# Seeding PSUM from ScalarE in both gates of an attention and gMLP kernel, with the scalings of weights and outputs on VectorE

## The chip, the core and the metric

The kernel runs on one core of a Trainium2 chip. The core has five engines that run side by side and meet through semaphores: TensorE (PE) multiplies matrices into PSUM, ScalarE (ACT) and VectorE (DVE) read and write PSUM and SBUF, GpSimd (POOL) works on SBUF, and SyncE (SP) issues most of the transfers. PSUM has eight banks of 128 x 512 float32. The metric is the device time of one execution in microseconds; lower is better.

## What is computed

Attention with a compressive memory over a layer-normalised input, added to the input; then a gated MLP over the layer-normalised sum, added again. The change lies in the second half, which is, cut to what matters:

```python
z = _gelu(jnp.einsum('bsd,df->bsf', x, w_in))        # x: 2048 x 1024, w_in: 1024 x 3584
z1 = z[..., :Fh].copy()                              # Fh = 1792
z2 = _layernorm(z[..., Fh:], axis=-1)
g = jnp.einsum('ts,bsf->btf', w_sp, z2) + b_sp[None, :, None]    # w_sp: 2048 x 2048
return jnp.einsum('bsf,fd->bsd', z1 * g, w_out)
```

So the "gate" is a product of the 2048 x 2048 matrix w_sp with z2, to which a bias per output token t is added, and which is then multiplied element by element with z1.

## The kernel before

**How the order comes about.** The program is written out once by Python code. Every call such as `act.activation(...)` or `pe.matmul(...)` goes through a recorder (lines 30 to 260), which appends it to the list of its engine and works out what it must wait for: results it reads, readers of what it overwrites, and for a PSUM bank any earlier access of another engine. Each engine then runs its own list strictly in the order recorded. A waiting instruction therefore holds up everything behind it on its engine. All instructions are issued at one line (L214), so the profile tells them apart by the names of their tiles.

**Stages.** Attention and the layer norms, then z2 and z1 (their input products, with gelu), then the first gate (`gate(0)`, output tokens 0 to 1023), four `out_unit`s that finish tokens 0 to 255, the second gate (`gate(1)`, tokens 1024 to 2047), and the output stage with the remaining tokens.

**The gate.** The product is done by a Strassen-Winograd scheme: seven block products where a plain 2 x 2 blocking needs eight. The weights are blocks of w_sp, called b11, b12, b21, b22, and their differences t1 to t4 (`sp_sum` in the first gate, `q_sum` in the second); the other operand is z2 in feature blocks of 128, of which `a_blk(i, j, g)` picks one, and sums of such blocks, SS[0] to SS[3] (`s_sum(1)` to `s_sum(4)`, DVE). Features are done in seven groups, g = 0 to 6. A product is eight matmuls of 128 x 128 by 128 x 512 into one bank. In the order of PE, a group has: t2 and t1, in groups 1 to 3 a p1 for a later group, t3, p2 of the next group, t4, b22. Banks rotate: three for p1/p2 (`g % 3`), two for t2, t3, t4 (`bb`), two for t1 and b22 (`bc`); bank 7 is left for sums of squares.

p1(g), the product with b11, is needed four times over. Before the change it goes this way:

- `copy1` (ACT) copies p1, scaled by `inv`, into `s1` (tile tmp_s) in SBUF; POOL adds the two halves of the bias row BROW to it and writes `s1b1` and `s1b2` (tile tmp_s1b).
- After t2, DVE's `stt` computes u2 = bank x inv + s1b2; after t3, u3 in the same way from the same bank (tile tmp_u). t3 adds on to the bank of t2, so it cannot start before u2 has read it, nor t4 before u3.
- The four outputs of a group are each a `stt` into VB, scaling a bank and adding u2, u3, s1b1 or BROW, followed by a multiplication with z1 (`out`), both on DVE. The first gate writes Z1T, the second Z1X.

`each(g, k)` with k = 0 to 3 are four places in each group where other work is put into the queues: in the first gate (`each0`) sums of squares of the gate's outputs (`z1_norm`) and of the output weights (`w_norm`), the loads of the second gate's blocks (`q_load`) and their scaling to float16 (`q_conv`); in the second gate (`each1`, from a table `jobs`) sums of squares of the finished outputs (`y0_norm`), their scale (`y0_scale`) and scaling (`y0_conv`), the scale of the output weights (`scale_w`), their loads (`ob_load`), scaling (`ob_scale`) and differences (`ob_sum`). The scales are powers of two that keep float16 in range.

**Between the gates**, `brow_sq` squares the new bias rows, `scale_y` derives YS and `INVY`, scales the rows by YS on ACT, and `q_conv` and `q_sum` prepare the remaining blocks.

**The output stage** uses the same scheme with seven matmuls a product: `o_p1(g)` is copied by ACT into a tile `ot`, POOL adds the residual to it three times (`o_adds`), `o_p2(g)` adds on to the same bank and `o_c11` evicts it. Before the change o_p2(0) follows o_p1(0) directly.

Of the kernel before, what the change touches and what calls it, by code (L numbers as in the profile page):

```python
# [262 lines left out]
def bass_sequential_preLN__memory_aug_infini_attn__mixer_gmlp__prompt_kernel(  # L263
# [24 lines left out]
    def tens(name, shape, dt, off):  # L288
        sz = int(np.prod(shape[1:])) * mybir.dt.size(dt)
        assert off % 32 == 0 and off + sz <= ARENA, (name, off, sz)  # L290
        t = nc.alloc_sbuf_tensor_at(name, list(shape), dt, offset=abase + off)
        R.space[t[:].tensor.name] = ("sbuf", off)
        return t

    class Bump:
# [4 lines left out]
        def __call__(self, name, shape, dt):  # L300
# [90 lines left out]
          for p, o in enumerate((162, 105))]  # L391
# [16 lines left out]
    SC = [b3("sc%d" % i, [128, 1], F32) for i in range(2)]  # L408
    INV = [b3("inv%d" % i, [128, 1], F32) for i in range(2)]
    TW, YS, INVY, SCW, INVO = [b3(k, [128, 1], F32) for k in ("tw", "ys", "invy", "scw", "invo")]  # L410
    SQY = tens("sqy", [128, 28], F32, 768)
    BSQ = tens("bsq", [128, 2], F32, 896)
    TMP = {k: tens("tmp_" + k, [128, L], F32, o * K)
           for k, o in zip(("s1", "s1b1", "s1b2", "u2", "u3"), (190, 192, 194, 196, 12))}
# [23 lines left out]
    def bank(b):  # L438
        return PS[:, b, :]
# [7 lines left out]
    free = []  # L447
# [768 lines left out]
        sp.dma_start(RAW1[k][:].rearrange("p j c n -> p j (c n)"), WSPT[Q4.index(k)])  # L1216

    def q_conv(k):
        if k == "b22":
            dve.tensor_single_scalar(BH1[k][:], RAW1[k][:], SC[0][:], ALU.mult)  # L1220
            return
        if k == "b21":
            dve.tensor_single_scalar(BH1[k][:, 0:2], RAW1[k][:, 0:2], SC[0][:], ALU.mult)
        for r in range(2 * (k == "b21"), 4):
            act.activation(BH1[k][:, r], RAW1[k][:, r], ACTF.Copy, scale=SC[0][:])
# [19 lines left out]
    def a_blk(i, j, g):  # L1245
        f = 896 * i + 128 * g
        return Z2H[:, 8 * j:8 * j + 8, f:f + 128]
# [8 lines left out]
        else:  # L1256
            dve.tensor_tensor(SS[:, 3], a_blk(0, 1, g), SS[:, 1], ALU.subtract)

    def gate(pr, seam=lambda: None, mid=lambda: None, each=lambda g, k: None):
# [4 lines left out]
        def prod(b, a, w, first):  # L1264
            for i in range(8):
                pe.matmul(bank(b), a[:, i, :], bh(w, i), start=(first and i == 0), stop=(i == 7),
                          skip_group_check=True)

        s1, s1b1, s1b2, u2, u3 = (TMP[k][:] for k in ("s1", "s1b1", "s1b2", "u2", "u3"))

        def stt(o, b, add):
            dve.scalar_tensor_tensor(o, bank(b), inv[:], add, ALU.mult, ALU.add)

        def out(v, g, i, t):
            dve.tensor_tensor(zo[:, g + 7 * i, t], v, Z1T[:, g + 7 * i, t], ALU.mult)

        def ss(k, g):
            if g < 7:
                s_sum(k, g)

        def p1(g):
            prod(g % 3, a_blk(0, 0, g), "b11", True)

        def copy1(g):
            act.activation(s1, bank(g % 3), ACTF.Copy, scale=inv[:])

        def p2(g):
            prod(g % 3, a_blk(0, 1, g), "b21", False)

        def c11(g):  # L1290
            stt(VB[:], g % 3, BROW[0][:])
            out(VB[:], g, 0, t1)

        p1(0)
        copy1(0)
        for o, k in ((s1b2, 1), (s1b1, 0)):
            (dve if pr else pool).tensor_tensor(o, s1, BROW[k][:], ALU.add)
        p1(1)
        p1(2)
        seam()  # L1300
        p2(0)
        c11(0)
        for g in range(7):
            bb, bc = 3 + g % 2, 5 + g % 2
            prod(bb, SS[:, 1], "t2", True)
            prod(bc, SS[:, 0], "t1", True)
            stt(u2, bb, s1b2)
# [9 lines left out]
            prod(bb, SS[:, 2], "t3", False)  # L1317
            if g < 5:
                copy1(g + 1)
                p2(g + 1)  # L1320
            elif g == 5:
                p1(6)
                copy1(6)
            else:
                p2(6)
            each(g, 1)
            stt(u3, bb, s1b2)
            stt(VB[:], bc, u3)
            out(VB[:], g, 1, t2)
            if not g:  # L1330
                ss(1, 1)
                ss(2, 1)
            if g < 6:
                pool.tensor_tensor(s1b2, s1, BROW[1][:], ALU.add)
            ss(3, g + 1)
            if g != 5:
                c11(min(g + 1, 6))
            prod(bb, a_blk(1, 1, g), "t4", False)
            each(g, 2)
            stt(VB[:], bb, s1b1)  # L1340
            out(VB[:], g, 1, t1)
            if g < 6:
                pool.tensor_tensor(s1b1, s1, BROW[0][:], ALU.add)
            prod(bc, SS[:, 3], "b22", False)
            stt(VB[:], bc, u2)
            out(VB[:], g, 0, t2)
# [82 lines left out]
    def on(g, k, f, *a):  # L1429
        todo1.setdefault((g, k), []).append((f, a))  # L1430
# [105 lines left out]

    def each0(g, k):
        z1_norm(g, k)
        for h, lo in ((1, 15), (0, 21)):
            for n in range(14):  # L1540
                if 4 * g + k == lo + n // 5:
                    w_norm(h, n)
            if 4 * g + k == lo + 2 and h:
# [6 lines left out]
        if (g, k) == (4, 0):  # L1550
            total(28, SQY, TOTY)
        if (g, k) == (6, 0):
            brow_in(1)
            q_load("b11")
            q_load("b12")
            q_conv("b11")
        if (g, k) == (6, 1):
            fin_load(units[1])
            w1_load(1)
            q_conv("b12")  # L1560
        if (g, k) == (6, 2):
# [14 lines left out]
    def scale_y():  # L1576
        power(YS)
        dve.tensor_tensor(INVY[:], INV[0][:], YS[:], ALU.mult)
        for k in range(2):
            act.activation(BROW[k][:], BROW[k][:], ACTF.Copy, scale=YS[:])  # L1580

    brow_sq()
    pool.tensor_tensor(TOT[:], TOTY[:], TW[:], ALU.mult)
    rot["banks"], rot["n"] = [0, 1, 2, 3], 0
    free.clear()
    q_sum("t1")
    for n, u in enumerate(units):
        out_unit(u, (lambda i: WO0[i // 7][:, i % 7, :]) if u[1] == 0 else
                 (lambda i: WO1[i // 7][:, i % 7, :]))
        if n == 0:  # L1590
            s_sum(1, 0)
            s_sum(2, 0)
        if n == 2:
            scale_y()
            q_conv("b21")
            q_sum("t3")
        if n == 1:
            q_conv("b22")
    q_sum("t2")
# [205 lines left out]
```

## Time and profile before

| | |
|---|---|
| median of three runs | 746.99 us (746.89 to 747.02) |
| the profiled execution | 747.36 us, of which its span (first to last instruction) 745.6 us |
| granted TensorE clock | 1.000 over the span |
| end of z1, start of the first gate | 483.9 us |
| first gate / units / second gate / output stage | 84.64 / 12.08 / 86.73 / 78.25 us |
| busy in the first gate: PE, DVE, ACT, POOL | 84.64, 68.03, 48.37, 19.43 us |
| busy in the second gate: PE, DVE, ACT, POOL | 85.36, 80.61, 44.32, 16.90 us |

The page lists groups of instructions as "out<-in xcount | busy us, mean ns | idle before, and what ended it". The timeline lists instructions as "start, duration, engine, line, what", in us from the span's start, with the idle time before an instruction and its releaser in brackets. Matmuls overlap, so a row's duration is longer than the distance to the next row; distances are read from start to start.

### The profile page before, as it was taken

To read this page: it belongs to the slowest core of one execution; us is meant where nothing else is said; L and a number is where in the kernel's file an instruction comes from. 1 tells how busy PE (TensorE), PEld (TensorE's weight loads), DVE (VectorE), ACT (ScalarE), POOL (GpSimd) and SP (SyncE) were. 2 spreads that over 40 slices of the span, in tenths; PEclk is the share of its full clock that TensorE was granted. 3 is DMA by queue.
4 is the path that set the end of the run, shared out by engine and by line. 5 is a ranking of instruction groups with operands and counts; after the bars stand their busy time and mean duration, and the time that the engine had idled before them with its cause. 6 is when DMAs were issued, how large, how long until landed. Compare 5 with 4: busy or idle time off the path is not lost.

```text
span 745.6 us, 13617 instructions
## 1 busy us (share of the span) xinstructions
PE 735.0 (99%) x5399; PEld 351.4 (47%) x5399; DVE 609.9 (82%) x1065; ACT 480.5 (64%) x656; POOL 307.7 (41%) x448
## 2 busy tenths in 40 slices
PE   8999999999999999999999999999999999999998
PEld 3454455545555445545554444444444444444444
DVE  5577889889988989879896777797885989987676
ACT  6777888888887888816886669846538687000000
POOL 2555456555654343110154899632220122224342
PEclk9999999999999999999999999999999999999999
DMA  9565668457635752644050037399638201031311
GB/s 295 178 171 121 140 143 179 130 148 165 171 99 162 250 177 58 178 120 128 29 141 1 1 57 127 68 193 189 200 117 307 71 22 36 1 114 63 106 57 57
DMA packets 148800, 92.65 MB, mean 124 GB/s; under 512 B 105984, under 2 KB 132864, under 8 KB 148224
## 3 DMA queue, kind: packets, MB, share of 16 engines
q1 hardware_dynamic: 147920, 91.00, 46.9%
q8 instruction: 42, 0.69, 0.4%
q10 hardware_dynamic: 816, 0.79, 0.3%
q14 instruction: 22, 0.18, 0.1%
HBM read 56.11 MB, written 12.58 MB: 92 GB/s over the span
## 4 chain that ended last, share of the span: by engine, by line
PE 84%; DVE 7%; ACT 3%; issue 3%; DMA 1%; POOL 1%; ACTq 0%; DVEq 0%; POOLq 0%
PE ps L214 84%; ACT ps L214 1%; DMA wv<-in_A_wv_dram 1%; DVE sqz L214 1%; DVE vb L214 1%; DVE stats L214 1%; ACT b12g L214 1%; DVE tmp_u L214 0%; ACT b11g L214 0%; DVE ss L214 0%; DVE z1x L214 0%; ACT e L214 0%; DVE hch L214 0%; POOL sz L214 0%; DVE tm L214 0%
## 5 line engine op out<-in xcount | busy, mean ns | idle before, releaser
L214 ACT ACTIVATE e<-ps 128x2048 bf16<-128x2048 f32 (+1 forms) x96 | 152.7, 1590 | 21.3 <-PE ps L214 20.6
L214 POOL TENSOR_SCALAR_AFFINE_SELECT e<-e 128x512 bf16<-128x512 bf16 x128 | 91.2, 726 | 123.1 <-ACT e L214 122.9
L214 POOL TENSOR_TENSOR tmp_s1b<-tmp_s,brow 128x512 f32<-128x512 f32 x26 | 33.9, 1305 | 104.5 <-DVE tmp_u L214 37.0
L214 PE MATMUL ps<-xnT,wk 128*128 128x512 bf16 x256 | 60.8, 380 | 0.6 <-ACT v L214 0.4
L214 PE MATMUL ps<-wv,xnT 128*128 128x512 bf16 x256 | 59.7, 380 | 1.3 <-DMA wv<-in_A_wv_dram 1.2
L214 PE MATMUL ps<-xnT,wq 128*128 128x512 bf16 x256 | 60.5, 379 | 0.0
L214 PE MATMUL ps<-wo,oT 128*128 128x512 bf16 x256 | 58.2, 380 | 0.8 <-DVE hch L214 0.8
L214 ACT ACTIVATE ot<-ps,invo 128x512 f32<-128x512 f32 x7 | 4.8, 687 | 70.6 <-PE ps L214 70.6
L214 POOL TENSOR_TENSOR ot<-ot,fin 128x512 f32<-128x512 f32 x21 | 27.9, 1352 | 47.1 <-ACT ot L214 47.1
L214 PEld LDWEIGHTS ps<-v,e 128*128 128x128 bf16 x1280 | 38.8, 96 | 14.0 <-issue 6.5
L214 PE MATMUL ps<-v,e 128*128 128x33 bf16 x1280 | 42.2, 178 | 0.0
L214 POOL TENSOR_TENSOR sz<-wzh 128x512 f16<-128x512 f16 x28 | 34.1, 1218 | 11.1 <-PE ps L214 11.1
L214 DVE BATCH_NORM_STATS2 zst<-z 128x6 f32<-128x448 bf16 x64 | 38.1, 609 | 0.0
L214 PEld LDWEIGHTS ps<-wo,oT 128*128 128x128 bf16 x256 | 24.0, 98 | 28.6 <-DVE hch L214 1.3
L214 PE MATMUL ps<-z2h,sy 128*128 128x512 f16 (+2 forms) x182 | 37.4, 363 | 0.0
L214 DVE TENSOR_TENSOR zt<-ps,zt 128x512 f32<-128x512 f32 x28 | 19.1, 686 | 22.1 <-PE ps L214 17.6
L214 PEld LDWEIGHTS ps<-xnT,wk 128*128 128x128 bf16 x256 | 22.6, 98 | 30.6 <-issue 4.5
L214 ACT ACTIVATE qk<-ps 128x512 bf16<-128x512 f32 x48 | 28.7, 598 | 12.9 <-PE ps L214 12.9
L214 PEld LDWEIGHTS ps<-wv,xnT 128*128 128x128 bf16 x256 | 23.2, 98 | 28.3 <-DMA wv<-in_A_wv_dram 1.9
L214 PE MATMUL ps<-qk 32*128 32x128 bf16 (+3 forms) x512 | 34.5, 302 | 0.7 <-DVE tm L214 0.5
L214 PEld LDWEIGHTS ps<-xnT,wq 128*128 128x128 bf16 x256 | 23.5, 98 | 22.9 <-issue 0.2
L214 ACT ACTIVATE z<-zp,inv 128x448 bf16<-128x448 f32 x28 | 18.6, 665 | 19.5 <-DVE zp L214 19.4
(284 smaller groups left out, 1712.7 us busy)
## 6 DMA issues: line engine op xcount, KB each, us to landing
nb<-in_B_w_in_dram SPq DMA_DIRECT2D x16, 448.0 KB, 4.1
nb<-in_B_w_sp_dram SPq DMA_DIRECT2D x14, 512.0 KB, 4.6
w_out<-in_B_w_out_dram SPq DMA_DIRECT2D x6, 896.0 KB, 5.9
xch<-in_A_x_dram SPq DMA_DIRECT2D x16, 256.0 KB, 4.6
xr<-in_A_x_dram SPq DMA_DIRECT2D x16, 256.0 KB, 3.9
out_dram<-hch SPq DMA_DIRECT2D x16, 256.0 KB, 2.4
w_spT<-stg SPq DMA_DIRECT2D x16, 256.0 KB, 4.2
out_dram<-fin SPq DMA_DIRECT2D x31, 128.0 KB, 1.7
```

The costliest lines, as they stand in the source:

```text
L214: ins = getattr(e, op.name)(*op.args, **op.kw)
```

## The change

In both gates the bias and the first product are no longer added outside PSUM. ACT writes a starting value into a bank (a seed), and every product accumulates on it (`start=False` throughout):

- `seed_a(g)`: BROW[0] times RINV into p1's bank, before p1(g). RINV is 1/INV[0], computed once in the z1 stage, so that the later scaling by inv gives the bias back; in the second gate INVY = INV[0] x YS scales it by YS as well, and the rows themselves are no longer scaled.
- `seed_b(g)`: p1's bank, seed included, copied to the bank of t2, t3 and t4.
- `seed_c(g)`: the difference of the two bias rows (`db`, computed once a gate by POOL) times RINV into the bank of t1 and b22.
- `copy_u(2, g)` and `copy_u(3, g)`: u2 and u3 become plain scaled copies on ACT. copy1, s1, s1b1 and s1b2 go.
- Of the four outputs of a group, the two of token half t1 become a single DVE instruction (bank x inv x z1); the two of half t2 stay a `stt` and a multiplication.
- The first two seeds of the first gate are issued in the z1 stage (`pre_seed`), into banks that are free by then. The gate's banks are taken from the list of free banks in their order (`perm`).
- In group 0 of the second gate the order of PE is t1, t2, p2(0), t3.
- All of `q_conv`, `ob_scale` and `y0_conv` move from ACT to DVE; `w_norm` is spread over more places (three for each instead of five) and begins one place earlier or later; the sum `total(28, SQY, TOTY)` moves from place (4, 0) to (4, 3); the scaling of b11 and b12 moves to (6, 2) and (6, 3); `q_sum("t3")` moves behind `s_sum(3, 0)`.
- In the output stage o_p2(0) and o_c11(0) move behind o_t4(0), as in the other groups.

```diff
+    RINV = tens("rinv", [128, 1], F32, 1024)
...
     def q_conv(k):
...
+        dve.tensor_single_scalar(BH1[k][:], RAW1[k][:], SC[0][:], ALU.mult)
...
+        def prod(b, a, w):
             for i in range(8):
+                pe.matmul(bank(b), a[:, i, :], bh(w, i), start=False, stop=(i == 7), skip_group_check=True)
...
+        def out(g, i, t, b, add=None):
+            o, z = zo[:, g + 7 * i, t], Z1T[:, g + 7 * i, t]
+            if add is None:
+                dve.scalar_tensor_tensor(o, bank(b), inv[:], z, ALU.mult, ALU.mult)
+            else:
+                dve.scalar_tensor_tensor(VB[:], bank(b), inv[:], add, ALU.mult, ALU.add)
+                dve.tensor_tensor(o, VB[:], z, ALU.mult)
...
+        def seed_a(g):
+            act.activation(bank(ba(g)), BROW[0][:], ACTF.Copy, scale=RINV[:])
+
+        def seed_b(g):
+            act.activation(bank(bb(g)), bank(ba(g)), ACTF.Copy)
+
+        def seed_c(g):
+            act.activation(bank(bc(g)), TMP["db"][:], ACTF.Copy, scale=RINV[:])
+
+        def copy_u(k, g):
+            act.activation(u(k, g), bank(bb(g)), ACTF.Copy, scale=inv[:])
...
+        for g in range(2 * (pr == 0), 3):
+            seed_a(g)
         p1(0)
...
+        pool.tensor_tensor(TMP["db"][:], BROW[1][:], BROW[0][:], ALU.subtract)
+        seed_b(0)
+        seed_c(0)
         p1(1)
         p1(2)
         seam()
+        if pr == 0:
+            p2(0)
+            out(0, 0, t1, ba(0))
         for g in range(7):
+            if pr and not g:
+                prod(bc(g), SS[:, 0], "t1")
+            prod(bb(g), SS[:, 1], "t2")
+            if g or not pr:
+                prod(bc(g), SS[:, 0], "t1")
+            else:
+                p2(0)
+            copy_u(2, g)
+            if pr and not g:
+                out(0, 0, t1, ba(0))
             if g == 0:
                 mid()
             ss(4, g)
             if g:
                 ss(1, g + 1)
                 ss(2, g + 1)
+            if g < 5:
+                seed_b(g + 1)
+            if g < 6:
+                seed_c(g + 1)
             if 1 <= g <= 3:
                 p1(g + 2)
+            if g < 4:
+                seed_a(g + 3)
             each(g, 0)
+            prod(bb(g), SS[:, 2], "t3")
             if g < 5:
                 p2(g + 1)
             elif g == 5:
                 p1(6)
             else:
                 p2(6)
+            copy_u(3, g)
+            if g == 5:
+                seed_b(6)
             each(g, 1)
+            out(g, 1, t2, bc(g), u(3, g))
...
+            prod(bb(g), a_blk(1, 1, g), "t4")
             each(g, 2)
+            out(g, 1, t1, bb(g))
+            prod(bc(g), SS[:, 3], "b22")
+            out(g, 0, t2, bc(g), u(2, g))
             each(g, 3)
...
+    on(13, 5, pre_seed)
+    on(13, 2, pre_seed)
...
+    gate(0, banks, seam, mid, each0)
...
     def ob_scale(k, h):
-        act.activation(ob_c(k, 4 * h, 4 + 3 * h), ob_c(k, 4 * h, 4 + 3 * h, Z2, WO0), ACTF.Copy, scale=SCW[:])
+        dve.tensor_single_scalar(ob_c(k, 4 * h, 4 + 3 * h), ob_c(k, 4 * h, 4 + 3 * h, Z2, WO0), SCW[:], ALU.mult)
...
     def y0_conv(n):
...
-            act.activation(Z1X[s], Z1T[s], ACTF.Copy, scale=YS0[:])
+            dve.tensor_single_scalar(Z1X[s], Z1T[s], YS0[:], ALU.mult)
...
+    gate(1, [banks[k] for k in (0, 3, 5, 1, 2, 4, 6)], each=each1)
...
-        if g and not end:
+        if not end:
             o_p2(g)
             o_c11(g)
```

More of the change, by code (lines that the diff above doesn't have):

```diff
@@ L413, in bass_sequential_preLN__memory_aug_infini_attn__mixer_gmlp__prompt_kernel @@
     TMP = {k: tens("tmp_" + k, [128, L], F32, o * K)
-           for k, o in zip(("s1", "s1b1", "s1b2", "u2", "u3"), (190, 192, 194, 196, 12))}
+           for k, o in zip(("db", "u20", "u21", "u30", "u31"), (190, 192, 194, 196, 12))}
     VB = tens("vb", [128, L], BF16, 61 * K)
@@ L1218, in q_conv @@
     def q_conv(k):
[L1219 to L1225, printed above, removed]
+        dve.tensor_single_scalar(BH1[k][:], RAW1[k][:], SC[0][:], ALU.mult)
     def q_sum(o):
@@ L1257, in s_sum, with gate @@
             dve.tensor_tensor(SS[:, 3], a_blk(0, 1, g), SS[:, 1], ALU.subtract)
-    def gate(pr, seam=lambda: None, mid=lambda: None, each=lambda g, k: None):
+    def gate(pr, perm, seam=lambda: None, mid=lambda: None, each=lambda g, k: None):
         inv, zo = (INV[0], Z1T) if pr == 0 else (INVY, Z1X)
@@ L1262, in gate, with ba, bb, bc @@
         bh = (lambda w, i: BH[w][:, i, :]) if pr == 0 else (lambda w, i: BH1[w][:, :, i, :])
-        def prod(b, a, w, first):
-            for i in range(8):
[L1266 to L1275, printed above, removed]
+        def ba(g):
+            return perm[g % 3]
+        def bb(g):
+            return perm[3 + g % 2]
+        def bc(g):
+            return perm[5 + g % 2]
+        def prod(b, a, w):
+            for i in range(8):
+                pe.matmul(bank(b), a[:, i, :], bh(w, i), start=False, stop=(i == 7), skip_group_check=True)
+        def u(k, g):
+            return TMP["u%d%d" % (k, g % 2)][:]
+        def out(g, i, t, b, add=None):
[5 more added lines that the diff above has]
+                dve.tensor_tensor(o, VB[:], z, ALU.mult)
         def ss(k, g):
@@ L1279, in ss @@
                 s_sum(k, g)
+        def seed_a(g):
[6 more added lines that the diff above has]
+            act.activation(u(k, g), bank(bb(g)), ACTF.Copy, scale=inv[:])
         def p1(g):
-            prod(g % 3, a_blk(0, 0, g), "b11", True)
-        def copy1(g):
-            act.activation(s1, bank(g % 3), ACTF.Copy, scale=inv[:])
+            prod(ba(g), a_blk(0, 0, g), "b11")
         def p2(g):
[L1288 to L1292, printed above, removed]
+            prod(ba(g), a_blk(0, 1, g), "b21")
+        for g in range(2 * (pr == 0), 3):
+            seed_a(g)
         p1(0)
-        copy1(0)
-        for o, k in ((s1b2, 1), (s1b1, 0)):
-            (dve if pr else pool).tensor_tensor(o, s1, BROW[k][:], ALU.add)
+        pool.tensor_tensor(TMP["db"][:], BROW[1][:], BROW[0][:], ALU.subtract)
+        seed_b(0)
+        seed_c(0)
         p1(1)
@@ L1300, in gate @@
         seam()
-        p2(0)
-        c11(0)
+        if pr == 0:
+            p2(0)
+            out(0, 0, t1, ba(0))
         for g in range(7):
[L1304 to L1307, printed above, removed]
+            if pr and not g:
[8 more added lines that the diff above has]
+                out(0, 0, t1, ba(0))
             if g == 0:
@@ L1313, in gate @@
                 ss(2, g + 1)
+            if g < 5:
+                seed_b(g + 1)
+            if g < 6:
+                seed_c(g + 1)
             if 1 <= g <= 3:
                 p1(g + 2)
+            if g < 4:
+                seed_a(g + 3)
             each(g, 0)
-            prod(bb, SS[:, 2], "t3", False)
+            prod(bb(g), SS[:, 2], "t3")
             if g < 5:
-                copy1(g + 1)
                 p2(g + 1)
@@ L1322, in gate @@
                 p1(6)
-                copy1(6)
             else:
                 p2(6)
+            copy_u(3, g)
+            if g == 5:
+                seed_b(6)
             each(g, 1)
-            stt(u3, bb, s1b2)
-            stt(VB[:], bc, u3)
-            out(VB[:], g, 1, t2)
+            out(g, 1, t2, bc(g), u(3, g))
             if not g:
@@ L1332, in gate @@
                 ss(2, 1)
-            if g < 6:
-                pool.tensor_tensor(s1b2, s1, BROW[1][:], ALU.add)
             ss(3, g + 1)
             if g != 5:
-                c11(min(g + 1, 6))
-            prod(bb, a_blk(1, 1, g), "t4", False)
+                out(min(g + 1, 6), 0, t1, ba(min(g + 1, 6)))
+            prod(bb(g), a_blk(1, 1, g), "t4")
             each(g, 2)
[L1340 to L1346, printed above, removed]
+            out(g, 1, t1, bb(g))
+            prod(bc(g), SS[:, 3], "b22")
+            out(g, 0, t2, bc(g), u(2, g))
             each(g, 3)
@@ L1440, in bass_sequential_preLN__memory_aug_infini_attn__mixer_gmlp__prompt_kernel @@
     on(2, 2, scale_end, 0)
+    on(3, 2, lambda: dve.reciprocal(RINV[:], INV[0][:]))
     for k, g, r in (("b11", 6, 3), ("b12", 6, 3), ("b22", 8, 3), ("b21", 12, 3)):
@@ L1451, in bass_sequential_preLN__memory_aug_infini_attn__mixer_gmlp__prompt_kernel, with pre_seed @@
     on(7, 3, brow_load, 0)
+    pre = []
+    def pre_seed():
+        pre.append([b for b in free if b < 7][len(pre)])
+        act.activation(bank(pre[-1]), BROW[0][:], ACTF.Copy, scale=RINV[:])
+    on(13, 5, pre_seed)
+    on(13, 2, pre_seed)
     seq2 = sorted((7 * q + OFF2[k], q, k) for q in range(len(G2)) for k in OFF2)
@@ L1538, in each0 @@
         z1_norm(g, k)
-        for h, lo in ((1, 15), (0, 21)):
+        for h, lo in ((1, 14), (0, 22)):
             for n in range(14):
-                if 4 * g + k == lo + n // 5:
+                if 4 * g + k == lo + n // 3:
                     w_norm(h, n)
-            if 4 * g + k == lo + 2 and h:
+            if 4 * g + k == lo + 4 and h:
                 w0_load(0)
@@ L1549, in each0 @@
             fin_load(units[0])
-        if (g, k) == (4, 0):
+        if (g, k) == (4, 3):
             total(28, SQY, TOTY)
@@ L1555, in each0 @@
             q_load("b12")
-            q_conv("b11")
         if (g, k) == (6, 1):
@@ L1559, in each0 @@
             w1_load(1)
-            q_conv("b12")
         if (g, k) == (6, 2):
@@ L1564, in each0 @@
             fin_load(units[3])
-    gate(0, seam, mid, each0)
+            q_conv("b11")
+        if (g, k) == (6, 3):
+            q_conv("b12")
+    assert full >= set(range(7)), full
+    banks = [b for b in free if b < 7]
+    assert sorted(banks) == list(range(7)) and banks[:2] == pre, (free, pre)
+    gate(0, banks, seam, mid, each0)
     q_load("b22")
@@ L1578, in scale_y @@
         dve.tensor_tensor(INVY[:], INV[0][:], YS[:], ALU.mult)
-        for k in range(2):
-            act.activation(BROW[k][:], BROW[k][:], ACTF.Copy, scale=YS[:])
     brow_sq()
     pool.tensor_tensor(TOT[:], TOTY[:], TW[:], ALU.mult)
-    rot["banks"], rot["n"] = [0, 1, 2, 3], 0
+    rot["banks"], rot["n"] = [banks[k] for k in (1, 2, 4, 6)], 0
     free.clear()
@@ L1595, in bass_sequential_preLN__memory_aug_infini_attn__mixer_gmlp__prompt_kernel @@
             q_conv("b21")
-            q_sum("t3")
         if n == 1:
@@ L1600, in bass_sequential_preLN__memory_aug_infini_attn__mixer_gmlp__prompt_kernel @@
     s_sum(3, 0)
+    q_sum("t3")
     OBG = {"b12": 0, "b22": 2, "t1": 1, "t2": 3, "t3": 4, "t4": 5}
@@ L1696, in each1 @@
             f(*a)
-    gate(1, each=each1)
+    gate(1, [banks[k] for k in (0, 3, 5, 1, 2, 4, 6)], each=each1)
     def o_prod(b, a, w, first, lo=0, hi=512):
@@ L1731, in bass_sequential_preLN__memory_aug_infini_attn__mixer_gmlp__prompt_kernel @@
     o_adds(0)
-    o_p2(0)
-    o_c11(0)
     ob_sum("t4", 3)
```

## The prediction

> **What bounds the kernel now.** First the page's busy times and its chain of waits.
>
> ```profile
> PE 735.0 (99%) x5399; PEld 351.4 (47%) x5399; DVE 609.9 (82%) x1065; ACT 480.5 (64%) x656; POOL 307.7 (41%) x448
> ...
> PE 84%; DVE 7%; ACT 3%; issue 3%; DMA 1%; POOL 1%; ACTq 0%; DVEq 0%; POOLq 0%
> ```
>
> TensorE (PE) is busy 99% of the span and 84% of the chain. The change removes no matmul, so it can win only PE's pauses in the stages it touches. Next the stage table: first gate, units between, second gate, output.
>
> ```profile
> 483.90:568.54 84.64, 84.64 (x395) 38.40 (x394) 68.03 (x106) 48.37 (x125) 19.43 (x16) 1.00 0.75 185
> 568.54:580.62 12.08, 12.08 (x57) 5.45 (x56) 7.39 (x9) 7.14 (x10) 2.64 (x5) 1.00 0.75 284
> 580.62:667.35 86.73, 85.36 (x395) 37.94 (x394) 80.61 (x135) 44.32 (x55) 16.90 (x15) 1.00 0.18 49
> 667.35:745.60 78.25, 74.40 (x358) 34.26 (x356) 53.04 (x72) 4.81 (x7) 27.85 (x21) 1.00 0.21 68
> ```
>
> After the length come PE, PEld, DVE, ACT, POOL. The first gate pauses nowhere; the second, with the same 49 products, takes 2.1 us longer, and VectorE (DVE) is busy 80.6 of its 86.7 us. PE's timeline gives the places.
>
> ```profile
> 592.74 1.89 PE L214 MATMUL ps<-b21g,z2h 128*128 128x512 f16 x8
> 595.54 1.90 PE L214 MATMUL ps<-t4g,z2h 128*128 128x512 f16 x8 [0.92 <-DVE tmp_u L214]
> ...
> 647.49 1.89 PE L214 MATMUL ps<-t1g,ss 128*128 128x512 f16 x8
> 649.82 1.90 PE L214 MATMUL ps<-t3g,ss 128*128 128x512 f16 x8 [0.44 <-DVE tmp_u L214]
> ...
> 667.35 1.67 PE L214 MATMUL ps<-w_out0h,z1x 128*128 128x512 f16 x7
> 669.81 1.69 PE L214 MATMUL ps<-w_out0h,z1x 128*128 128x512 f16 x7 [0.78 <-ACT ot L214]
> ```
>
> Unhindered products start 1.727 us apart (seven matmuls: 1.511). From start to start the pauses are 595.54-592.74-1.73 = 1.07; 649.82-647.49-1.73 = 0.60; five small ones at 590.98 to 660.43, together 0.40; and 669.81-667.35-1.51 = 0.95. Sum 3.0 us: the most that can be won. In the gate they come from u2/u3 (tmp_u), which DVE writes late; in the output stage from o_p2(0), which needs o_p1(0)'s copy at once.
>
> **The change, part by part.** Prices are rows of this profile:
>
> ```profile
> L214 ACT ACTIVATE ps<-ps 128x512 f32<-128x512 f32 x14 | 8.2, 585 | 1.4 <-PE ps L214 1.4
> L214 ACT ACTIVATE tmp_s<-ps,inv 128x512 f32<-128x512 f32 x7 | 4.8, 685 | 28.6 <-POOL tmp_s1b L214 19.0 <-PE ps L214 9.6
> L214 DVE SCALAR_TENSOR_TENSOR vb<-ps,invy,brow 128x512 bf16<-128x512 f32 x7 | 5.2, 741 | 0.0
> L214 ACT ACTIVATE z1x<-z1T,ys 128x1344 f16<-128x1344 bf16 x8 | 10.6, 1402 | 3.1 <-DVE ys L214 3.1
> ...
> L214 DVE TENSOR_SCALAR b21g<-b21q,sc x1: 747/747/747, 581.3 to 581.3; 128x2048 f16<-128x2048 bf16 x1
> ...
> L214 DVE TENSOR_SCALAR b22g<-b22q,sc x1: 1281/1281/1281, 579.1 to 579.1; 128x4096 f16<-128x4096 bf16 x1
> ```
>
> *ScalarE (ACT).* Out: 14 copy1 x 0.69, b11g/b12g 8 x 1.13, half of b21g 2.3, two brow 1.4, output weights 4 x 1.99 + 4 x 1.56, y0_conv 8 x 1.40: 48 us. In: 28 copy_u x 0.69, 14 seed_b x 0.585 (row ps<-ps), 14 seed_a and 14 seed_c: 47 us. A scaled copy from SBUF into PSUM is in no row; nearest are 0.60 (square of w_out into PSUM) and 0.71 (brow scaled in SBUF). I take 0.69, as for a scaled copy from PSUM; the span moves by 0.1 either way.
>
> *DVE.* Out: 28 tmp_u x 0.75, 28 of 56 gating multiplies x 0.42, two s1b adds x 0.68: 34 us. In: b11g, b12g 2 x 1.28, b21g 0.53 more, output weights, y0_conv. Rows of 2048 and 4096 elements (0.747, 1.281) lie on 0.213 + 0.00026 a piece, so 1536 cost 0.61 and 1344 cost 0.56: 4 x 0.75 + 4 x 0.61 + 8 x 0.56 = 9.9. Net DVE is 21 us lighter. POOL loses 26 adds.
>
> y0_conv's 7 rows of 192 are the one shape without a row: below, 0.56; above, 1.61 (one element per 1/0.96 ns, as 512 cost 0.68 in f32, plus the constant). I take 0.56: same operation and types, even runs. The Trainium skill, "VectorE: DVE Perf Modes", section "What auto-detection actually checks", grants the two-port modes to a single-source operation in SBUF when the outer counts are even or equal in source and destination; 7 and 7 are equal, so by it the low price holds. No row here shows an odd count.
>
> *First gate* (PE never waits, so this can only lose). The two early seeds sit where ACT idles 0.3 to 1.0 us between gelus (478.8 to 482.1). ACT then holds per group of 12.08 us: 3 seeds and 2 copies 2.9 us, 8 squares x 0.755 = 6.0. The tightest is group 0: t2 ends 492.54, +0.26 copy_u2, three seeds, two squares, copy_u3 done 497.2, t4 due 497.7. w_out's second load starts some 2 us later (547.7 for 545.6; DMA ran 4 us), lands near 552; its squares begin 555.5, and six of them end before copy_u2(6) at 560.2; t3(6) is due 561.63. Were it as slow as the slowest such load (8.6 us) the margin would be 0.1. On SP's queue nothing is held by that: the next entry, w1_load(0), waits for a product until 554.7 anyway. In group 4 the moved small matmul and eight squares leave 0.18 at its bank and 0.25 at t4(4). b11g now stands in DVE's queue before out(6,1,t1), b12g behind the gate's last output: their loads land 564.9 and 568.4, b11g runs 566.1 to 567.4, out(6,1,t1) is there at 568.1, and the unit's fourteenth matmul, which reads it, comes at 571.3. The reciprocal is one step of 0.16. Cost 0.
>
> *Units.* The brow rows no longer wait for YS, so ACT writes three seeds at 572 to 574. DVE ends b12g at 571.2 and t1g at 573.5 (576.7 before); t2g at 583.8, t3g at 586.6; due 587.5 and 591.0. Cost 0.
>
> *Second gate, group 0.* PE: p1 x 3 to 585.80, t1, t2 to 589.25, p2 to 590.98, t3, p2(1) to 594.46, then t4. DVE waits for p2(0) with out(0,0,t1): 591.24 to 591.99; ss4, then t4g 592.5 to 594.8. ACT: copy_u2 589.5, seed_b, seed_c, then seed_a(3), which must wait for that same output's bank until 592.02, two y0_norm x 0.96, copy_u3 594.53 to 595.22. t4 starts 595.28: **0.81 late** instead of 1.07; were ACT free at once, t4g alone would make it 0.35. b22(0), due 597.0, needs scw and out(0,1,t2): 596.75. t2(1), due 598.73, needs SS[1] at 598.54. Both pass by 0.1 to 0.2.
>
> *Group 2.* t2 starts 610.82, so scale's small matmul is at 616.0; DVE's small steps end 618.24 (1.95 us, as before), then a weight scaling, two y0_conv, a sum (0.53 + 2 x 0.48 + 0.60), then out(2,1,t2) to 621.09. b22(2), due 621.21, passes by 0.06. The gate's other groups keep 0.7 us or more, as ACT is idle when u2 and u3 are due.
>
> *Output.* o_p2(0) now follows o_t4(0): its 0.95 goes. o_t3(0) then meets f12's read within 0.01 us (POOL's first add, 1.15; 1.5 in later groups): 0 to 0.4 lost, I take 0.
>
> Sum: 3.0 - 0.8 = **2.2 us** off (2.7 with t4 at 0.35; 1.0 if group 2 loses 0.3, a slower POOL add 0.4 and t4 0.5 more). Profiled: span 745.6 - 2.2 = 743.4, time 747.36 - 2.2 = 745.2. The three runs' median lies 0.37 under that execution: **744.8**.
>
> A rule against the change: the skill's "SBUF — State Buffer", section "Who interferes with whom", has a DVE two-port operation, or one with two SBUF inputs, exclude GpSimd until it ends. The trace agrees (t1h sums of 1024 took up to 1.64 instead of 0.68 beside POOL's work), and here it bears on the rival of the output stage.
>
> **Rivals.** *Gain eaten by small delays* (within 0.2%, that is 1.5 us, about what can be told apart here): the margins of 0.01, 0.06 and 0.13 fail. DVE once paused 0.91 on issue (556.7); such a pause in group 2 costs 0.9, a POOL add held by the weight sums of gate group 6 costs 0.4: 746.1. Or y0_conv runs at two elements a cycle, 0.91 each: b22(2) 0.6 and b22(3) 1.1 late, 746.5. For: so many tight places; against: the same reckoning gives the pauses of before to 0.2 us.
>
> *Slower:* y0_conv at one element a cycle. Four per group stand before out(2,..) and out(3,..), whose banks b22(2), b22(3) need. At 1.61 group 2 brings 2 x 1.05 - 0.06 = 2.0; group 3 takes six of them less its idle 1.0: 5.3. Then 744.8 + 7.3 = 752.1; it turns slower than before above 0.97 each. For: no row has this shape; against: every contiguous bf16 scaling on DVE ran at four per cycle.
>
> *No effect on the gate:* ACT's queue binds as DVE's did (copy_u behind squares in more groups): only the 0.95 of the output stage is won, 746.0; against it, ACT's idle of 1.4 to 6 us before most copies.
>
> **How the numbers follow.** Forecast 0.66 (gain over 1.5 us), eaten or no effect 0.20, slower 0.14. The range runs from 744.1 (t4 0.35 late, 0.2 of reckoning) to 747.5, taking in both rivals within 0.2% and the two-per-cycle price; the slow rival and the rest below make up what is left out. Forecast's own range: 744.1 to 745.5.
>
> **What would show it.** Second gate's window 85.5 us with one pause near 0.8 at t4(0), released by ACT; no tmp_u releaser; y0_conv near 0.56 on DVE; o_t2(0) right behind o_p1(0); first gate still 84.64. Wrong if z1x shows 0.9 or more, if b22(2) or b22(3) waits for DVE, or if t3/t4 of the first gate wait for ACT.

## The result, and the profile after

The changed kernel takes 744.17 us (median; 743.84 to 744.65) against 746.89 us of the kernel before in the same series: ratio 0.9965, 95% interval 0.9954 to 0.9977. That is 2.7 us less, and the interval allows 1.7 to 3.4; 744.8 was forecast. The profiled execution took 744.07 us, with a span of 742.4. First the page's busy times and its chain of waits.

```profile
PE 730.3 (98%) x5333; PEld 351.7 (47%) x5399; DVE 582.3 (78%) x1026; ACT 478.6 (64%) x684; POOL 276.4 (37%) x424
...
PE 87%; DVE 8%; ACT 2%; issue 1%; DMA 1%; POOL 0%; DVEq 0%
```

VectorE (DVE) and POOL are some 30 us lighter each, ScalarE (ACT) holds as much as before; none of this tells where 2.7 us went. The stage table does (first gate, units, second gate, output; after the length PE, PEld, DVE, ACT, POOL):

```profile
483.26:567.90 84.64, 84.64 (x394) 38.37 (x394) 50.10 (x79) 60.78 (x148) 2.28 (x3) 1.00 0.73 186
567.90:579.98 12.08, 11.97 (x55) 5.48 (x56) 10.61 (x14) 3.25 (x7) 4.09 (x6) 1.00 0.84 292
579.98:665.30 85.32, 84.83 (x395) 38.25 (x394) 68.41 (x116) 32.68 (x60) 1.30 (x3) 1.00 0.18 48
665.30:742.40 77.10, 74.23 (x358) 34.29 (x356) 52.35 (x72) 4.81 (x7) 27.85 (x21) 1.00 0.21 69
```

First gate and units are as long as before to the hundredth, although DVE is 18 us lighter and ACT 12 us heavier in the first gate: no pause there, nothing to win. The second gate went from 86.73 to 85.32. PE's timeline shows the pause that is left, and the output stage without one (a name such as t4(0) is the product with t4 in group 0):

```profile
592.09 1.89 PE L214 MATMUL ps<-b21g,z2h 128*128 128x512 f16 x8
594.48 1.90 PE L214 MATMUL ps<-t4g,z2h 128*128 128x512 f16 x8 [0.49 <-ACT tmp_u L214]
...
665.30 1.67 PE L214 MATMUL ps<-w_out0h,z1x 128*128 128x512 f16 x7
666.82 4.70 PE L214 MATMUL ps<-z2h,z1x 128*128 128x512 f16 x21
671.35 1.67 PE L214 MATMUL ps<-w_out0h,z1x 128*128 128x512 f16 x7
```

t4(0) starts 594.48 - 592.09 - 1.73 = 0.66 us late and waits for ACT, no longer for DVE; the other pauses of the gate are gone. In the output stage t2, t1 and t3 follow o_p1(0) 1.52 us after its start, where before there was a gap of 0.95 in front of o_p2(0). From the start of the output stage to that of its last product it is 72.54 us, before 73.49.

The new work, as groups of instructions (count, busy time in us, mean ns):

```profile
L214 ACT ACTIVATE tmp_u<-ps,invy 128x512 f32<-128x512 f32 x14 | 9.6, 686 | 44.2 <-PE ps L214 44.2
...
L214 ACT ACTIVATE ps<-brow,rinv 128x512 f32<-128x512 bf16 x14 | 9.4, 679 | 0.7 <-DVE z1x L214 0.7
...
L214 DVE TENSOR_SCALAR z1x<-z1T,ys 128x1344 f16<-128x1344 bf16 x8 | 4.5, 607 | 0.0
```

Ahead of 13 of the 14 copies of the second gate ACT had been idle, 44.2 us in all, waiting for the product itself: these copies are made as soon as they can be. The one that isn't is copy_u3(0), on which t4(0) waits. It stands right behind the two y0_norm squares of group 0, of which this is the second:

```profile
592.91 0.84 ACT L214 ACTIVATE z1T<-z1T 128x768 bf16<-128x768 bf16 x1
...
593.75 0.67 ACT L214 ACTIVATE tmp_u<-ps,invy 128x512 f32<-128x512 f32 x1
```

A y0_conv shows 0.607 us, not far from the lower of the two bounds that were open (0.56 and 1.61).

So the span's 3.2 us are 1.41 (second gate) + 0.95 (output) + 0.64 + 0.20. The 0.64 had arisen before the first gate began (483.26 against 483.90), the 0.20 lies behind the last product. In the profiles of all kernels shown here the first gate began between 482.30 and 484.01, in no order of their edits: on average at 483.08 in the three with the gates of before (before, e1, e6) and at 483.09 in the eleven with those of after. So nothing shows that the change has a part in the 0.64, and what follows is read from stages.

### The profile page after: what moved, and what is told of

Its sections match the earlier page's. It is cut to its first block, busy times and chain, and to the rows that moved or that the text cites. A ratio compares the mean times of both kernels' runs of the same rounds, so it can differ in the third digit from the quotient of the medians.

```text
span 742.4 us, 13475 instructions
## 1 busy us (share of the span) xinstructions
PE 730.3 (98%) x5333; PEld 351.7 (47%) x5399; DVE 582.3 (78%) x1026; ACT 478.6 (64%) x684; POOL 276.4 (37%) x424
## 4 chain that ended last, share of the span: by engine, by line
PE 87%; DVE 8%; ACT 2%; issue 1%; DMA 1%; POOL 0%; DVEq 0%
PE ps L214 87%; DVE stats L214 2%; DVE sqz L214 1%; DMA wv<-in_A_wv_dram 1%; DVE hch L214 1%; DVE otok L214 1%; DVE pqk L214 1%; ACT e L214 1%; DVE ta L214 0%; DVE rd L214 0%; DVE rdm L214 0%; DVE etmp L214 0%; POOL sz L214 0%; DVE tm L214 0%; DVE sq L214 0%
## 5 line engine op out<-in xcount | busy, mean ns | idle before, releaser
L214 PE MATMUL ps<-xnT,wq 128*128 128x512 bf16 x226 | 54.0, 379 | 1.6
L214 ACT ACTIVATE tmp_u<-ps,invy 128x512 f32<-128x512 f32 x14 | 9.6, 686 | 44.2 <-PE ps L214 44.2
L214 ACT ACTIVATE ps<-ps 128x512 f32<-128x512 f32 (+1 forms) x42 | 23.9, 568 | 14.0 <-PE ps L214 14.0
```

The source lines that it names most:

```text
L214: ins = getattr(e, op.name)(*op.args, **op.kw)
```

## The experiments

Theory: the gain is the sum of single pauses of PE, which end because the copies u2 and u3 come from an engine that is free when they are due, and because o_p2(0) stands elsewhere. Rivals: it is the seeding as such; ACT's queue binds instead; everything hangs on one stage. Windows are from the second gate's first product to the output stage's first, without any pause 84.66.

| kernel | second gate, us | output to last product, us | median, us |
|---|---|---|---|
| before | 86.73 | 73.49 | 746.2 to 746.9 (each series) |
| changed | 85.32 | 72.54 | 744.17 |
| e1 move of o_p2(0) alone | 86.71 | 72.54 | 745.84 |
| e2 without that move | 85.33 | 73.49 | 744.89 |
| e3 t4(0) freed | 84.66 | 72.54 | 742.68 |
| e4 second gate's copies on DVE | 90.67 | 72.54 | 748.14 |
| e5 scalings back on ACT | 88.96 | 72.54 | 747.60 |
| e6 scalings alone to DVE | 92.69 | 73.49 | 752.72 |
| e7 y0_conv in pieces | 87.36 | 72.54 | 745.94 |
| e8 first gate's copies on DVE | 85.32 | 72.54 | 743.94 |
| e9 norms later | 85.29 | 72.54 | 743.45 |
| e10 t4g earlier | 85.31 | 72.54 | 744.16 |
| e11, e12 longer pause | 86.30, 91.18 | 72.53, 72.54 | 744.69, 748.55 |

**The two places, each alone (e1, e2).** The edit of e1, on the kernel before; e2 is its reverse on the changed kernel:

```diff
     o_adds(0)
-    o_p2(0)
-    o_c11(0)
     ob_sum("t4", 3)
...
-        if g and not end:
+        if not end:
             o_p2(g)
```

> The kernel before, with one edit: o_p2(0) and o_c11(0) leave their place ahead of the output loop and stand in group 0 behind the t4 product, as in the other groups. Both gates stay as they were. Theory (the gain is the sum of single PE pauses, each won by itself): o_p2(0)'s pause of 0.95 us goes, the four pauses of the second gate stay (2.07 us), so 746.9 - 0.95 = 745.9 us. Rival (one train of work: the pause comes back at the next wait of the output stage, o_t3(0), whose f12 buffer POOL has just written): 746.5 to 746.9 us.

> The changed kernel, with o_p2(0) and o_c11(0) put back directly behind o_p1(0). Theory: the gates keep their gain (2.07 - 0.66 = 1.4 us) and the output stage gets its pause of 0.95 us back: 744.2 + 0.95 = 745.1 us, the second gate's window still 85.3 us. Rival (the gates gave nothing, the output stage gave all): 746.9 us. Rival (the o_p2(0) move gave nothing): 744.2 us.

Measured 745.84 (ratio 0.9988, 0.9979 to 0.9996) and 744.89 (0.9974, 0.9965 to 0.9984). In e1 the gate keeps its 86.71 and the output stage drops by exactly 0.95; in e2 it is the other way round. The two parts add up, and neither rival holds.

**Who copies (e4, e8).** e4, and with `not pr` e8:

```diff
         def copy_u(k, g):
-            act.activation(u(k, g), bank(bb(g)), ACTF.Copy, scale=inv[:])
+            if pr:
+                dve.tensor_single_scalar(u(k, g), bank(bb(g)), inv[:], ALU.mult)
+            else:
+                act.activation(u(k, g), bank(bb(g)), ACTF.Copy, scale=inv[:])
```

> The changed kernel, with the 14 copies copy_u2/copy_u3 of the second gate made by DVE (same scaling, PSUM to SBUF) instead of ACT; the first gate and all else stay. Theory (the copies' move to ACT is what pays in the gate): DVE gets 14 x 0.67 = 9.4 us on top of 68.4 in a window of 85.3. copy_u3(0) then stands behind t4g and the steps of scale_w (done 595.4), t4(0) starts near 596.1 for a due time of 593.8: 2.3 late instead of 0.66. b22(2) is some 0.6 late (a copy more in front of out(2,1,t2)), group 3 some 0.5. Together 744.2 + 1.6 + 0.6 + 0.5 = 746.9 us, within 0.7. Rival (it doesn't matter who copies, seeding the banks is what pays): 744.2 us.

> The changed kernel, with the 14 copies copy_u2/copy_u3 of the first gate made by DVE instead of ACT; the second gate stays. Theory (the first gate had no pause to win, and has none that depends on who copies): DVE is busy 50.1 of 84.6 us there and gets 9.4 more, PE still waits for nothing, from the first gate's start to the second's 96.7 us as in all runs so far: 744.2, at most 744.6 us. Rival (the copies on ACT are what keeps the first gate without pauses): 745.5 us or more, with t3 or t4 of the first gate waiting for DVE.

e8: 743.94, from the first gate's start to the second's still 96.72. There it doesn't matter who copies. e4: 748.14 (1.0018, 1.0007 to 1.0030), slower than before and beyond what was expected (746.9, within 0.7). PE's timeline of e4:

```profile
595.58 2.33 PE L214 MATMUL ps<-t4g,z2h 128*128 128x512 f16 x8 [2.12 <-DVE tmp_u L214]
597.70 3.19 PE L214 MATMUL ps<-b22g,ss 128*128 128x512 f16 x8
600.73 1.89 PE L214 MATMUL ps<-t2g,ss 128*128 128x512 f16 x8
...
623.80 1.90 PE L214 MATMUL ps<-b22g,ss 128*128 128x512 f16 x8 [0.40 <-DVE vb L214]
631.25 1.90 PE L214 MATMUL ps<-t3g,ss 128*128 128x512 f16 x8 [0.37 <-DVE tmp_u L214]
635.21 1.90 PE L214 MATMUL ps<-t4g,z2h 128*128 128x512 f16 x8 [0.34 <-DVE tmp_u L214]
```

The pauses stand where they were expected: t4(0) 2.28 late from start to start (2.3 expected), b22(2) 0.56 (0.6), group 3 0.52 + 0.49 (0.5). The seeds are all there; without the copies on ACT the gate is slower than before. Two things exceed the expectation. 0.9 us are further waits (half of group 3's, and group 4). And t4(0) took 597.70 - 595.58 = 2.12 and b22(0) 3.03 instead of 1.73: 1.7 us without a wait, which e12 takes up. Six of the twelve executions had a granted clock of 1.000 and so not this loss; their median, 747.5, is within what was expected, and above the 746.73 of the kernel before too.

**The scalings (e5, e6).** e5 puts y0_conv and ob_scale of the changed kernel back on ACT; e6 takes the same two lines of the kernel before to DVE:

```diff
     def ob_scale(k, h):
-        dve.tensor_single_scalar(ob_c(k, 4 * h, 4 + 3 * h), ob_c(k, 4 * h, 4 + 3 * h, Z2, WO0), SCW[:], ALU.mult)
+        act.activation(ob_c(k, 4 * h, 4 + 3 * h), ob_c(k, 4 * h, 4 + 3 * h, Z2, WO0), ACTF.Copy, scale=SCW[:])
...
-            dve.tensor_single_scalar(Z1X[s], Z1T[s], YS0[:], ALU.mult)
+            act.activation(Z1X[s], Z1T[s], ACTF.Copy, scale=YS0[:])
```

> The changed kernel, with y0_conv and ob_scale (the scalings of y0 and of the output weights) given back to ACT, as before the change; seeds, copies and all else stay. Theory (the two halves of the change need each other: ACT can take the copies because it gave the scalings away): ACT gets 8 x 1.40 and 4 x 1.99 + 4 x 1.56, 25 us. In groups 0 to 2 its queue then holds 13.8, 15.7 and 13.4 us (copies and seeds 3.4 a group, y0_norms, scalings) for the 12.1 us that PE takes for a group; copy_u2 and copy_u3 stand behind them, with some 1 to 2 us to spare: t3 and t4 of groups 1 to 3 wait for ACT, 6.7 - 2 = 4.7 us together, in group 3 (8.2 us) it ends. 744.2 + 4.7 = 748.9, between 747 and 751 us. Rival (the scalings were moved for nothing, ACT has room as its share of busy time of 64% says): 744.2 us, or less, as DVE is 10 us lighter.

> The kernel before, with y0_conv and ob_scale alone moved from ACT to DVE. Theory: without the copies' move DVE, 80.6 us busy in a second gate of 86.7, gets 9.9 us more and binds. In group 2 the weight scaling (0.53) and two y0_conv (1.05) stand before u3(2), which makes t4(2) some 1.5 late; in group 3 six more y0_conv come before u3(3), some 2 more; the weight scalings of groups 0 and 1 (2.5) add 1 to 2. Together 4 to 6 us: 746.9 + 5 = 752, between 750 and 753.5 us. Rival (DVE's 6.1 us of idle time in this window take the scalings in): 746.9 us.

e5: 747.60 (1.0009, 1.0000 to 1.0018), the gate 3.6 us longer than in the changed kernel where 4.7 were expected. e6: 752.72 (1.0079, 1.0062 to 1.0096), 6.0 us slower than before where 5 were expected. In e5 PE waits for ACT, and ACT's timeline says behind what:

```profile
617.95 1.90 PE L214 MATMUL ps<-t3g,ss 128*128 128x512 f16 x8 [1.42 <-ACT tmp_u L214]
```

```profile
614.51 0.83 ACT L214 ACTIVATE z1T<-z1T 128x768 bf16<-128x768 bf16 x1
...
615.34 1.99 ACT L214 ACTIVATE z2h<-z,scw 128x2048 f16<-128x2048 bf16 x1
617.23 0.66 ACT L214 ACTIVATE tmp_u<-ps,invy 128x512 f32<-128x512 f32 x1
```

The copy u2(2) stands behind a square and a weight scaling of 1.99 us; PE waits for neither of them, only for the copy. ACT is busy only 55.5 of the 89.0 us of this gate, and yet it is what PE waits for. In e6 DVE is busy 88.95 of 92.69, and beside t4(0), t3 or t4 waits for tmp_u in each of the groups 2 to 5. So moving the scalings alone loses 6.0 us, the rest of the change without them loses 0.9 by the medians, and together they win 2.7.

e4 and e6 also tell what the seeds do. In both DVE makes the copies and the scalings, but e4 has the seeds and e6 hasn't. DVE is busy 77.59 us in the second gate of e4, 88.95 in that of e6, and the gate of e4 is 2.0 us shorter, 3.7 without the 1.7 us of the low clock. So the seeds take work off DVE, which makes room for the scalings there. These two kernels differ in the order of group 0 and in q_conv's engine as well, so the 3.7 us are not the seeds' share alone.

**How near DVE is (e7).**

```diff
-        for h in range(2):
-            s = (slice(None), slice(7 * (n // 2), 7 * (n // 2) + 7), slice(256 + 384 * (n % 2) + 192 * h, 448 + 384 * (n % 2) + 192 * h))
+        for h in range(8):
+            s = (slice(None), slice(7 * (n // 2), 7 * (n // 2) + 7), slice(256 + 384 * (n % 2) + 48 * h, 304 + 384 * (n % 2) + 48 * h))
```

> The changed kernel, with each y0_conv (7 rows of 192 columns) cut into four of 48 columns: the same values by 32 instructions instead of 8. On DVE an instruction follows the next after 0.175 us and 0.00026 a column (0.525 for 1344), so four pieces of 336 take 1.05 instead of 0.525. Theory (the gate's margin by the prediction's rule: b22(2) has 0.06 to spare behind two y0_conv, b22(3) stands behind all eight): b22(2) is 2 x 0.525 - 0.06 = 1.0 late; out(3,1,t2) comes 8 x 0.525 = 4.2 later (its first half done at 635.8 for a due time of 632.5 in the changed kernel's times), so b22(3) is 3.3 late in all: 744.2 + 3.3 = 747.5 us, slower than before by 0.6. Rival (DVE, 80% busy in this gate, takes 4.2 us more without a wait of PE): 744.2 us.

Measured 745.94 (0.9991, 0.9982 to 1.0001), where 747.5 was expected. DVE's timeline of the changed kernel, then of e7:

```profile
617.91 1.13 DVE L214 TENSOR_SCALAR z1x<-z1T,ys 128x1344 f16<-128x1344 bf16 x2
618.96 0.68 DVE L214 TENSOR_TENSOR z2h<-z2h,w_out0h 128x1024 f16<-128x1024 f16 x1
```

```profile
617.66 1.85 DVE L214 TENSOR_SCALAR z1x<-z1T,ys 128x336 f16<-128x336 bf16 x8
619.43 0.68 DVE L214 TENSOR_TENSOR z2h<-z2h,w_out0h 128x1024 f16<-128x1024 f16 x1
```

```profile
620.83 1.90 PE L214 MATMUL ps<-b22g,ss 128*128 128x512 f16 x8 [0.50 <-DVE vb L214]
634.28 1.90 PE L214 MATMUL ps<-b22g,ss 128*128 128x512 f16 x8 [1.19 <-DVE vb L214]
```

Eight pieces hold DVE for 619.43 - 617.66 = 1.77 us, two whole ones for 1.05. A piece costs 0.22, not 0.26, so the price was too high: 0.72 more per pair instead of 1.05. With 0.72 the places and the sum of the reckoning fit. b22(2) is 0.67 late from start to start, which leaves a margin of 0.05 (0.06 was forecast), and b22(3) 1.35, together 2.02 for a window longer by 2.04.

**The pause that is left (e3, e9, e10).** e3 has both edits, e10 the first alone, e9 the second alone:

```diff
     q_sum("t3")
+    q_sum("t4")
...
-    job(0, 0, q_sum, "t4")
...
-        job(r // 7, (r % 7) // 2, y0_norm, r)
+        job(r // 7, max((r % 7) // 2, r < 7), y0_norm, r)
```

> The changed kernel with two edits that concern only the one pause that is left in the second gate (t4(0), 0.66 us): the sum t4g is written ahead of the gate, in the 4.67 us in which DVE idles before out(0,0,t1), and the two y0_norm squares that stand in ACT's queue before copy_u3(0) go behind it. Theory: both bounds on t4(0) (copy_u3(0) done at 594.42, t4g done at 594.10, t4(0) due at 593.82 in the changed kernel's times) are gone, the pause falls to 0 and the window of the second gate to 84.66: 744.2 - 0.66 = 743.5 us. Rival (the pause is handed on to b22(0) or t2(1), which DVE feeds with little to spare): 744.0 to 744.2 us.

> The changed kernel, with only the second of the two edits that freed t4(0): the two y0_norm squares go behind copy_u3(0) in ACT's queue; t4g stays where it is. Theory (two bounds on t4(0), ACT's copy at 594.42 and DVE's t4g at 594.10 in the changed kernel's times): copy_u3(0) is done some 1.8 earlier, t4(0) then waits for t4g, 0.66 - 0.32 = 0.34 late, the second gate's window is 85.0: 743.8 us. Rival (ACT's queue alone was the bound): pause 0, window 84.66, 743.5 us.

> The changed kernel, with only the first of the two edits: t4g is summed ahead of the gate, in DVE's idle time; the two y0_norm squares stay before copy_u3(0). Theory: ACT's copy still ends at 594.42, t4(0) still starts 0.66 late, window 85.32: 744.2 us, no change from the changed kernel. Rival (t4g, which stood in the way of DVE's next steps, was the true bound, and the releaser that the trace names only came last by chance): window 84.66 to 85.0, 743.5 to 743.8 us.

e3: 742.68 (0.9947, 0.9935 to 0.9959), the fastest here; its second gate has no pause:

```profile
579.26:663.92 84.66, 84.66 (x395) 38.31 (x394) 68.47 (x116) 32.62 (x60) 1.30 (x3) 1.00 0.18 49
```

The window won 0.66 over the changed kernel; the other 0.8 of the medians' difference is outside it (its first gate began 0.7 earlier, in code that is the same). e10 changed nothing, as expected. e9 was expected to win 0.32 in the window and won 0.03. That its median, 743.45, is the figure of its rival is chance: the rival was a pause of 0 in a window of 84.66, and in its profile the first gate began at 482.44, 0.8 us earlier than in the changed kernel's. Its PE timeline:

```profile
593.42 1.89 PE L214 MATMUL ps<-t4g,z2h 128*128 128x512 f16 x8 [0.26 <-DVE tot L214]
595.29 1.90 PE L214 MATMUL ps<-b22g,ss 128*128 128x512 f16 x8
597.07 1.90 PE L214 MATMUL ps<-t2g,ss 128*128 128x512 f16 x8
```

t4(0) is 0.42 late, now on DVE's account, and what it gained is lost again at once: b22(0) starts 1.87 after it and t2(1) 1.78 after that, 0.14 and 0.05 more than a product takes. DVE runs t4g (its row ends at 593.28; `tot` is DVE's next step), the steps of the weight scale and only then out(0,1,t2), whose read of the bank ends at 595.23 and for which b22(0) waits. The kernel is held here by two engines that end nearly together; in the window each edit alone is worth next to nothing (0.03 and 0.01), both together the whole 0.66.

**What a pause costs (e11, e12).** In e11 three, in e12 five of the y0_norm squares stand before copy_u3(0), instead of two:

```diff
-        job(r // 7, (r % 7) // 2, y0_norm, r)
+        job(r // 7, 0 if r < 5 else (r % 7) // 2, y0_norm, r)
```

> The changed kernel, with one more y0_norm square (three instead of two) in ACT's queue before copy_u3(0); nothing else moves. This sizes a pause of PE by itself: copy_u3(0) ends 0.97 us later, t4(0) starts 0.66 + 0.97 = 1.63 late. Theory (a pause costs its length as long as the granted clock stays at 1.00, as in the run with a pause of 1.90): 744.2 + 0.97 = 745.1 us, granted clock 1.000 in nearly all executions. Rival (every pause of this kind lets the clock fall to 0.50 for 3.4 us, at 1.7 us more, as happened behind the pause of 2.28): 746.8 us.

> The changed kernel, with five y0_norm squares instead of two in ACT's queue before copy_u3(0). copy_u3(0) ends 2.91 us later, t4(0) starts 0.66 + 2.91 = 3.57 late. Theory (a long pause costs its length and in most executions also the 1.70 us that 3.4 us at half the clock cost behind the pause of 2.28, which showed in half of that kernel's executions): 744.2 + 2.9 = 747.1 us in executions with a clock of 1.000, 748.8 us in the others, and the others are more than half; the median is 748.8 us. Rival (the fall of the clock has nothing to do with the pause): 747.1 us, with a lowered clock in about 1 of 10 executions, as in the kernel before.

The pauses came out at 1.63 and 3.57 as set. e11: 744.69 (0.9972, 0.9963 to 0.9982), window 86.30, 0.98 longer, no execution of ten below a granted clock of 0.999. e12: 748.55 (1.0020, 1.0007 to 1.0033); four of its ten executions at 1.000 took 746.4 to 747.4, four at 0.998 took 748.4 to 748.8, two at 0.995 took 749.3 and 750.7. Stretches of one microsecond in e4, with the granted clock in the third column from the end, show what such a number is made of:

```profile
594.00:595.00 1.00, 0.00 (x0) 0.00 (x0) 0.44 (x3) 0.97 (x3) 0.49 (x1) 1.00 1.17 262
...
597.00:598.00 1.00, 1.00 (x4) 0.29 (x2) 0.96 (x2) 0.97 (x4) 0.00 (x0) 0.50 0.07 17
598.00:599.00 1.00, 1.00 (x4) 0.31 (x3) 1.00 (x3) 0.16 (x2) 0.00 (x0) 0.50 0.53 122
...
600.00:601.00 1.00, 1.00 (x6) 0.38 (x4) 0.75 (x3) 0.28 (x1) 0.00 (x0) 0.84 0.00 0
```

In e4 the clock falls to one half some 1.3 us after PE has started again, for about 3.4 us; that is the 1.7 us that e4 lost beyond its waits. In the profiled execution of e12 (0.995) it fell at 597.3, while PE was still idle, and was low for 6.8 us; t4(0) and b22(0) took 2.9 us more:

```profile
597.00:598.00 1.00, 0.00 (x0) 0.00 (x0) 0.00 (x0) 1.00 (x4) 0.00 (x0) 0.65 0.00 0
```

```profile
598.14 3.60 PE L214 MATMUL ps<-t4g,z2h 128*128 128x512 f16 x8 [3.41 <-ACT tmp_u L214]
```

From the start of PE's idle time to the fall it was 3.5 us in e4 and 2.6 in e12; two cases give no rule for the moment. The Trainium skill, "TensorE: Matmul & The Clock Gate", section "What's actually happening", has the two states, half and full, and a window of some 3.4 us; the trace agrees. The Trainium skill, same page, section "Why this matters for your kernels", asks for no gap of PE above about 3 us. Here less was enough: behind 2.12 us idle, six of twelve executions of e4 took 748.4 to 750.4 us against 746.7 to 747.9 of the other six. After 1.47 us (ten executions of e11) and 1.74 us (four of e6) it didn't show.

The pause isn't the only occasion. In the four series of the experiments six of 78 executions of the kernel before had a granted clock of 0.997 as well and took 748.5 to 749.3, though its profile shows no gap of PE above 1.24 us anywhere, and so had one execution each of e1, e2 (0.998) and e7 (0.997). No profile fell on one of them, so what lowered the clock there stays open. Pauses of 0.5 to 1 us, which this change is about, cost their own length.

## Why the prediction was right

- **What can be won lies in PE's pauses, at most 3.0 us:** right. Windows and e1, e2 return 1.41 and 0.95; with e3 the two stages give 2.07 + 0.95 = 3.02. (The median of e3 lies 4.05 under that of the kernel before in its series; 1.0 of it is outside the two stages.)
- **First gate and units 0:** right, 96.71 or 96.72 from start to start in every kernel here; e8 shows that the place of the copies is free there. The 2.9 us that the prediction takes for three seeds and two copies aren't the sum of its prices (3.3), but they fit from start to start: 2.32 + 0.57 us in group 0, as an instruction begins some 0.1 us before the row ahead of it ends.
- **o_p2(0), 0.95, and no new wait at o_t3(0):** right (e1, e2). The stall of the f12 buffer and of POOL's adds did not show: POOL is busy 27.85 us in the output stage before and after. The Trainium skill, "SBUF — State Buffer", section "Who interferes with whom", under which it was weighed, has DVE's two-port operations and GpSimd exclude each other.
- **t4(0) 0.81 late on ACT:** right in place and releaser, mis-sized by 0.15: it was 0.66. Counted from the gate's start, copy_u3(0) ended at 14.44 instead of 14.60. 0.05 of it came with DVE's output; 0.13 because two y0_norms held ACT 1.79 us, not 2 x 0.96, as the copy began before the second one's read-out had ended; the seed took 0.04 more than counted, the copy 0.02 less.
- **The lower bound for t4(0), 0.35, and with it a gain of 2.7:** wrong as a bound. e9 made that case: 0.42, and the gain went into b22(0). That the medians differ by 2.7 is chance; t4(0) was 0.66 late. I had both dates, b22(0) due at 597.0 and ready at 596.75, but let b22(0)'s due time stand while t4(0) moved ahead of it by 0.46; its spare of 0.25 was a spare only as long as t4(0) was late.
- **y0_conv 0.56 on DVE, the slow rival from 0.97:** right. 0.607 us by its row, and 0.525 from one start to the next: the odd count of rows keeps it far from the 0.91 of two elements a cycle, though the row is 0.05 above the line of the even shapes. The Trainium skill, "VectorE: DVE Perf Modes", section "What auto-detection actually checks", lets the two-port modes stand where outer counts are equal; the trace agrees. e7, at 0.89 each, ended 0.8 us under the kernel before, so the turning point isn't contradicted.
- **b22(2) with 0.06 to spare:** right; e7 measured 0.05.
- **ACT's queue doesn't bind:** right, because of the scalings (e5). Seeds took 0.68 (0.69 taken), the copies 0.69.
- **DVE 21 us lighter:** mis-sized, it is 27.6 (609.9 to 582.3). The rule that the prediction names as one against the change worked for it. Between 480 and 680 us, 24 of the 112 gating multiplies and z2 sums of the kernel before took longer than the others, a multiply up to 0.70 us instead of 0.42, and all 24 ran beside a POOL instruction; in the changed kernel, without POOL's 26 adds, none of 84 did.
- **The sum:** 2.2 forecast, 2.36 in the two stages, 2.7 in the medians. The 0.15 is t4(0). The rest, 0.4, lies outside the two stages and within the scatter of the start; the profiles show no part of the change in it. The stages alone give about 744.6, well inside the range of 744.1 to 747.5; that the median came within 0.1 of its lower end is scatter.

Not tried alone: seeding with the copies on DVE and the scalings on ACT. What the seeds are worth by themselves is therefore not shown. They don't carry the gain alone (e4 has them and is slower than before), nor are they worth nothing (e4 against e6).

## What to carry to other kernels

Look for the pauses of the engine that is busy 98%, from start to start, and look up what stands in front of the missing value on the engine that makes it; shares of busy time (ACT 62% in e5) say nothing about that. Work that is due at once belongs on an engine whose queue holds little in front of it, and long work without a date has to leave that queue first: half of such an exchange can lose more than the whole wins. When two engines end nearly together in front of a wait, a bound for one alone is not a gain: move the due times of all later waits along before counting it.

## What the runs showed of the hardware

With 2.1 us of idle time of PE in six of twelve executions (e4), with 3.4 us in six of ten (e12), the granted clock came out below 0.999, against six of 78 of the kernel before. In the two that were profiled it stood at 0.50 for 3.4 and 6.8 us, which cost 1.7 and 2.9 us beyond the pause. With 1.5 and 1.7 us idle none of 14 executions showed it (e11, e6).

On DVE an instruction that needn't wait starts 0.08 to 0.1 us before the row of the one ahead of it ends: eight pieces of 336 columns, 0.303 us each by the profile, took 1.77 us in a row, so short instructions are cheaper than their rows.

A DVE multiply of two SBUF operands of 512 columns took 0.42 us, and up to 0.70 beside an add on POOL.
